# A 32-byte pool ahead of everything else on the right side of SBUF

## The chip, the core and the metric

The kernel runs on one core of a Trainium2 chip. The metric is device time in microseconds (us) of one execution. A core has five engines with queues of their own: TensorE (PE; its weight loads are shown apart as PEld), VectorE (DVE), ScalarE (ACT), GpSimd (POOL) and SyncE (SP, which issues nearly all DMAs here). On-chip memory, SBUF, is addressed by partition (128 of them) and by byte within the partition. A TensorE product has two operands in SBUF: the *stationary* one, which a LDWEIGHTS loads ahead of it (128 columns at most), and the *moving* one, which is streamed through (up to 512 columns here). In the profile's names `out<-a,b` of a MATMUL, a is the moving operand and b the stationary one.

## What is computed

One transformer block with adaptive layer norm over 2048 tokens of width 512: a sliding-window attention of 32 heads of 16 (window 256), then a gated feed-forward layer of inner width 1792.

```python
mod = (_silu(c) @ w_mod).reshape(c.shape[0], 6, 1, -1)
sa, ca, ga, sb, cb, gb = ...
h = _layernorm(x, axis=-1) * (1 + ca) + sa
x = x + ga * _A_ref(h, A_wqkv, A_wo)      # softmax(q k^T / 4, 0 <= i - j < 256) v, @ wo
h = _layernorm(x, axis=-1) * (1 + cb) + sb
x = x + gb * _B_ref(h, B_w1, B_w3, B_w2)  # (silu(h @ w1) * (h @ w3)) @ w2
```

## The kernel before

Everything is float32. To multiply at the fast rate, most operands are cut into a high and a low part of type float32r, and a product is three TensorE products: high by high, low by high, high by low. Nearly all products stream 512 columns past 128 stationary ones.

The work goes in four stages:

- Until about 95 us: layer norm, transposes, the value projection (line 703: stationary `hT`, the normed input; moving `wvh`/`wvl`, the weights) and the first query and key projections.
- Until about 467 us: attention, in 32 units (8 query-key blocks of a group of heads times 4 blocks of 512 tokens). Query and key projection is line 518 (stationary `wq`, moving `hT`), the scores for the running maximum line 574 and the scores proper line 931 (both operands in the tile `ring`), the product with the values line 892.
- Until about 539 us: the output projection (line 1315: stationary `o` or `x1b`, moving `wo`), the second layer norm and its transposes.
- The rest: the feed-forward layer. It is run in two halves of 1024 tokens and seven passes each, 14 passes in all. A pass makes two times seven products of the up and gate projection by a Strassen-like scheme (line 1579; six TensorE products of 512 columns each, so 84 in a pass: stationary the pass's weights, moving the tiles `b`) and eight products of the down projection (line 1673; six each, so 48 in a pass: stationary the gated activations, moving `w2`).

The order of each engine's instructions is fixed before the program runs: a planner in the kernel (class `Sched`, with tables of offsets) deals the operations out, and they are issued in that order on each engine. Places in SBUF don't enter into it.

SBUF is filled from two sides. Pools without `side` grow from the low addresses, pools with `side="right"` from the top down. Within a pool each tile begins on a multiple of 32 bytes. The right side holds the pool `a1` (opened first, at the top), and below it `hp` with `hT`, later replaced by `xp`. In the built program the large tiles then begin as follows, as bytes modulo 128 (and modulo 512) of their partition:

| tiles | side | used as | mod 128 | mod 512 |
|---|---|---|---|---|
| `ring`, `vS`, `b`, `w`, `w2`, `t`, `g`, `e` | left | scores, values, feed-forward | 64 | 448 |
| `wvh`, `wvl`, `pt`, `sm`, `jb`, `os` | left | value weights, probabilities | 64 | 64 or 448 |
| `hT`; later `x1a`, `x1b`, `wo`, `o` | right | normed input; residual, weights, attention output | 96 | 96 |
| `qk0`..`qk2`, `qkr`, `wq00`..`wq11`, `wqr` (pool `a1`) | right | queries, keys, their weights; later the gated activations | 96 | 96 |
| `junk` (pool `a1`) | right | unread output of line 581 | 32 | |

A column of a moving operand and a block of 128 stationary columns always begin a multiple of 512 bytes into these tiles, so the table's byte is that of both operands of every product of lines 518, 574, 703, 931, 1315, 1579 and 1673.

The weights of the feed-forward passes sit in two sets of two tiles, used in turn (`load_w`: `s = (half * NP + p) % 2`). Set 0 is `w` in the pool `fp`, on the left; set 1 takes over the places of `wo` and `o` in `xp`, on the right (`second_open`), and is shown by the profile under these names. So seven of the 14 passes have their up-projection weights on the left and seven on the right, while the moving tiles `b` are on the left. In the down projection the stationary activations lie in `a1` on the right under the names `wq`, `qk`, `qkr` (in the last pass half of them in `e` on the left), and the moving `w2`, or in the last pass `w`, is on the left.

The two lines around the change, 411 and 412, open the pool of PSUM and the first pool of the right side.

Of the kernel before, what the change touches and what calls it, by code (L numbers as in the profile page):

```python
# [8 lines left out]
F32 = mybir.dt.float32  # L9
# [9 lines left out]
P = 128  # L19
# [349 lines left out]
def block_kernel(ctx: ExitStack, tc: tile.TileContext, x, wqk, wv, wo, w13, w2, c, crow, wmod, wmodt, out):  # L369
# [39 lines left out]
        return hT[:, i, k, lo:lo + n]  # L409

    psA = ctx.enter_context(tc.tile_pool(name="psA", bufs=1, space=PSUM))
    a1 = ctx.enter_context(tc.tile_pool(name="a1", bufs=1, side="right", reuse_waits="tile"))

    def ps(b):
# [1395 lines left out]
```

## Time and profile before

| | before |
|---|---|
| three runs, us | 956.42, 956.73, 955.26 |
| median, us | 956.42 |
| the profiled execution: time, us | 956.27 |
| its span, first to last instruction, us | 954.6 |
| granted TensorE clock | 0.998 |
| busy, share of the span: DVE, ACT, POOL | 77%, 59%, 52% |
| mean DMA rate over the span | 148 GB/s |

The profile gives busy time by engine, a chain of work that ended last (followed back from the last instruction, each step to what released it), groups of instructions by line and tile, and busy time in chosen windows. The ends of matmuls are modelled, and a product's shown length overlaps the next one's (389 ns are shown where products follow each other every 226.7), so how fast products follow each other is read from the chain, whose pieces abut. A piece is shown as its start, its length and `engine tile line xN`, all in us.

### The profile page before, as it was taken

Reading aid. Unit: us, or ns where it says so; the run is one execution under the profiler, and the core shown is the slowest. Engines: PE = TensorE matmul, PEld = TensorE weight load, DVE = VectorE, ACT = ScalarE, POOL = GpSimd, SP = SyncE. Lnnn points to the kernel's source line nnn. Section 1 sums busy time; section 2 is a strip of 40 time slices with the busy share of each in tenths; the row PEclk is TensorE's granted clock in tenths of the full one; section 3 lists DMA queues with packets and bytes.
Section 4 is the critical chain, followed back from the end, with each engine's and each line's share of the span. In section 5 each row is a group of like instructions: output and inputs, shape, how many; then the busy total and the mean of one; then the engine's idle time right before and its main releaser. Section 6 shows DMA issues by size and latency. Waiting matters only on the chain.

```text
span 954.6 us, 17091 instructions
## 1 busy us (share of the span) xinstructions
PE 937.3 (98%) x5296; PEld 714.9 (75%) x5296; DVE 734.3 (77%) x2065; ACT 561.1 (59%) x1263; POOL 498.9 (52%) x721
## 2 busy tenths in 40 slices
PE   8999999999999999998999999999999999999998
PEld 4678777777777677775688788888888888888886
DVE  8884989898989898998468765666679766667555
ACT  6533878787878787876779833433456333433230
POOL 3230877787878686867544655444866222221320
PEclk9999999999999999999999999999999999999999
DMA  9521444444544444437893555466684421322002
GB/s 327 191 73 40 132 170 146 147 145 147 167 159 146 146 146 145 135 129 232 240 277 101 176 162 191 137 185 221 221 279 144 149 82 57 99 84 76 23 23 88
DMA packets 81561, 141.64 MB, mean 148 GB/s; under 512 B 10555, under 2 KB 23227, under 8 KB 81470
## 3 DMA queue, kind: packets, MB, share of 16 engines
q1 hardware_dynamic: 81180, 140.29, 45.4%
q8 instruction: 42, 0.69, 0.3%
q14 instruction: 49, 0.40, 0.1%
q10 hardware_dynamic: 290, 0.27, 0.1%
HBM read 85.73 MB, written 34.61 MB: 126 GB/s over the span
## 4 chain that ended last, share of the span: by engine, by line
PE 86%; POOL 4%; DVE 3%; DMA 3%; ACT 2%; issue 1%; SPq 1%; POOLq 0%; ACTq 0%; DVEq 0%
PE st L1579 12%; PE mx L1579 10%; PE pj L518 8%; PE mx L574 7%; PE st L931 7%; PE mx L1673 7%; PE po L892 7%; PE st L1673 5%; PE pj L1579 3%; PE po L1579 3%; PE mx L703 2%; PE po L1673 2%; PE st L1315 2%; PE pj L1673 2%; PE mx L1315 2%; PE st L703 2%
## 5 line engine op out<-in xcount | busy, mean ns | idle before, releaser
L581 DVE CUSTOM_DVE_ANT_0 junk<-mx,mskq 128x384 bf16<-128x384 f32 (+1 forms) x482 | 242.1, 528 | 23.8 <-PE mx L574 22.3
L931 PE MATMUL st<-ring 100*128 100x384 f32 (+2 forms) x484 | 146.2, 343 | 1.0 <-ACT pt L952 0.4
L574 PE MATMUL mx<-ring 96*128 96x384 f32 (+2 forms) x482 | 144.6, 340 | 1.7 <-ACT pt L943 0.6
L959 POOL TENSOR_SCALAR_AFFINE_SELECT pt<-pt 128x256 f32<-128x256 f32 x268 | 108.7, 408 | 51.7 <-ACT pt L952 38.3
L518 PE MATMUL pj<-hT,wq 128*128 128x512 f32 x384 | 132.1, 403 | 0.0
L952 ACT ACTIVATE pt<-st 128x256 f32<-128x256 f32 x255 | 91.4, 387 | 36.6 <-DVE st L949 28.5
L574 PEld LDWEIGHTS mx<-ring 96*128 96x128 f32 x482 | 88.0, 189 | 31.1 <-DVE mt L581 21.1
L931 PEld LDWEIGHTS st<-ring 100*128 100x128 f32 x484 | 90.2, 189 | 18.8 <-issue 6.7
L1623 POOL TENSOR_TENSOR t<-t,t 128x512 f32<-128x512 f32 x28 | 41.6, 1487 | 115.5 <-DVE t L1611 108.4
L892 PE MATMUL po<-pt,vS 128*17 128x256 f32 (+2 forms) x1408 | 97.4, 387 | 2.7 <-ACT os L999 1.1
L536 POOL TENSOR_TENSOR qk<-qkr,qk 128x512 fp32r<-128x512 f32 x64 | 82.9, 1295 | 10.4 <-ACT qkr L524 9.0
L1170 POOL TENSOR_TENSOR w<-w,w 128x512 fp32r<-128x512 f32 (+2 forms) x35 | 51.1, 1471 | 59.0 <-ACT w L1169 58.5
L1611 DVE TENSOR_TENSOR t<-st,t 128x512 f32<-128x512 f32 x55 | 37.9, 690 | 51.4 <-PE st L1579 38.5
L518 PEld LDWEIGHTS pj<-hT,wq 128*128 128x128 f32 x384 | 71.3, 189 | 7.7 <-issue 0.9
L949 DVE COPY_PREDICATED st<-later,st 128x128 f32<-128x128 uint8 x255 | 68.8, 292 | 7.9 <-PE st L931 4.7
L892 PEld LDWEIGHTS po<-pt,vS 128*17 128x17 f32 x1408 | 32.3, 96 | 48.5 <-issue 19.3
L1579 PE MATMUL st<-b,w 128*128 128x512 f32 x234 | 59.1, 391 | 0.0
L943 ACT ACTIVATE pt<-st 128x384 f32<-128x384 f32 (+2 forms) x113 | 47.1, 433 | 14.9 <-DVE st L939 13.7
L976 POOL TENSOR_SCALAR_AFFINE_SELECT sm<-sm 128x256 f32<-128x256 f32 x109 | 42.1, 409 | 24.1 <-ACT sm L966 20.0
L1579 PE MATMUL mx<-b,w 128*128 128x512 f32 x204 | 51.7, 391 | 0.0
L1579 PEld LDWEIGHTS st<-b,w 128*128 128x128 f32 x234 | 43.9, 188 | 9.5
L1651 ACT ACTIVATE qkr<-g 128x512 fp32r<-128x512 f32 x13 | 8.2, 633 | 66.5 <-DVE g L1607 66.5
(349 smaller groups left out, 2139.7 us busy)
## 6 DMA issues: line engine op xcount, KB each, us to landing
ring<-qk SPq DMA_DIRECT2D x192, 128.0 KB
o_dr<-os SPq DMA_DIRECT2D x32, 256.0 KB
w<-wsum SPq DMA_DIRECT2D x14, 512.0 KB
w<-w2g SPq DMA_DIRECT2D x14, 512.0 KB
jb<-in_w SPq DMA_DIRECT2D x24, 256.0 KB
vS<-in_wmodt SPq DMA_DIRECT2D x22, 256.0 KB
wraw<-in_w SPq DMA_DIRECT2D x7, 768.0 KB
w<-wraw SPq DMA_DIRECT2D x14, 384.0 KB
```

Source lines behind the costliest of these rows:

```text
L518: nc.tensor.matmul(v["ps"], WQ[g][w][:, n // 3], hTp(i, n // 3, b * BT, BT), start=(n == 0), stop=(n == 3 * KC - 1))
L536: nc.gpsimd.tensor_tensor(out=v[n], in0=v["raw"], in1=v[1].bitcast(F32), op=ALU.subtract)
L574: nc.tensor.matmul(v[i][:, :n], queries(NS, a, gq, 1), keys(NS, hh, a, k0, gq + 1 - k0), start=True, stop=True)
L581: nc.vector.tensor_tensor_reduce(out=junk[:, :n], in0=v[i][:, :n], in1=mskq[:, 3 * P - n:], scale=1.0, scalar=-3e38, op0=ALU.add, op1=ALU. ...
L892: nc.tensor.matmul(po[32 * i:32 * i + DH + 1, qb * P:(qb + nq) * P], vS[:, kb, 4 * g + i], pts[i // 2][:, i % 2, c0:c0 + nq], start=first, ...
L931: nc.tensor.matmul(ps[:, :nq], keys(NM, hh, a, kb, 1), queries(NM, a, kb, nq), start=True, stop=not plus)
L949: nc.vector.copy_predicated(ps[:, 0], later, ps[:, 2])
L952: nc.scalar.activation(pt_of(j, a)[:, hh, :2], v[j, a, hh][:, :2], AF.Exp, scale=SCALE)
L959: nc.gpsimd.affine_select(out=pt[:, :, 2 * m], in_=pt[:, :, 0], **w)
L1170: sch.op(eng, lambda: on_eng(eng).tensor_tensor(out=lo(), in0=src(), in1=hi().bitcast(F32), op=ALU.subtract), tt(eng, n), key, kl + kh, kl ...
L1579: nc.tensor.matmul(ps(bk), WT[s, n][w][:, col], BB[t, k][r], start=start and c == 0, stop=stop and c == 5, skip_group_check=True)
L1673: nc.tensor.matmul(ps(bk), tiles[hk + (h,)][:, i * P:(i + 1) * P], w2_of(last, y, f), start=(m == 0), stop=(m == 5))
```

## The change

Ahead of `a1` a pool named `edge` is opened on the right side, with one tile of 8 float32 numbers, 32 bytes in each partition. Nothing reads or writes it.

```diff
     psA = ctx.enter_context(tc.tile_pool(name="psA", bufs=1, space=PSUM))
+
+    ctx.enter_context(tc.tile_pool(name="edge", bufs=1, side="right")).tile([P, 8], F32, name="edge")
     a1 = ctx.enter_context(tc.tile_pool(name="a1", bufs=1, side="right", reuse_waits="tile"))
```

Every tile of the right side moves down by 32 bytes: from 96 to 64 modulo 128 for the large ones, and from 32 to 0 for `junk`. The left side stays where it is. No instruction, no order and no wait on a semaphore changes, only the addresses of right-side operands. The large tiles of both sides then begin at byte 64 modulo 128. Modulo 512, the right side goes from 96 to 64, so that a right-side tile stands 128 bytes from `b`, `w` and `ring`, where it stood 160 from them; `hT` stands 0 bytes from `wvh` and `wvl`, where it stood 32 from them. Line numbers of the changed kernel are larger by two behind line 411.

## The prediction

> **What bounds the kernel now.** First the page: how busy TensorE is, and how much of the chain of waits is its own.
>
> ```profile
> PE 937.3 (98%) x5296; PEld 714.9 (75%) x5296; DVE 734.3 (77%) x2065; ACT 561.1 (59%) x1263; POOL 498.9 (52%) x721
> PE 86%; POOL 4%; DVE 3%; DMA 3%; ACT 2%; issue 1%; SPq 1%; POOLq 0%; ACTq 0%; DVEq 0%
> ```
>
> TensorE leaves some 17 us of the span idle, so a change that moves no instruction can gain much only by making TensorE's products follow each other faster. Where it is fully busy is read from windows (length, busy us and count by engine, granted clock, DMA share, GB/s):
>
> ```profile
> 25.00:95.00 70.00, 69.08 (x316) 51.52 (x314) 51.11 (x143) 30.20 (x50) 13.09 (x11) 1.00 0.30 96
> 200.00:300.00 100.00, 99.33 (x773) 71.91 (x765) 91.23 (x390) 79.85 (x228) 75.97 (x140) 1.00 0.47 151
> 600.00:700.00 100.00, 100.00 (x440) 81.11 (x439) 67.27 (x87) 40.47 (x65) 52.71 (x53) 1.00 0.63 206
> 700.00:800.00 100.00, 100.00 (x433) 81.07 (x432) 75.03 (x95) 48.43 (x79) 41.95 (x26) 1.00 0.43 143
> 800.00:905.00 105.00, 105.00 (x455) 85.09 (x455) 69.24 (x93) 36.22 (x57) 24.73 (x18) 1.00 0.21 64
> ```
>
> In the feed-forward layer TensorE has no idle time, at full clock, and no other engine is above 75% (the third busy column is DVE's). In attention DVE is at 91% too. So the feed-forward layer ends when TensorE is through, and the pace of one product is what counts there. That pace stands in the chain of waits. Its pieces around 694 us, where a pass with weights on the right ends and one with weights on the left begins:
>
> ```profile
> 690.26 1.40 PE st L1579 x6
> 694.46 1.39 PE st L1579 x6
> 695.85 1.37 PE pj L1579 x6
> 697.22 1.36 PE mx L1579 x6
> 698.58 1.36 PE po L1579 x6
> 710.83 1.40 PE pj L1673 x6
> ```
>
> Six products of the same shape take 1.40 us on one side of 694 us and 1.36 after it: 233.3 and 226.7 ns each. The groups by tile say what differs (mean ns behind the busy time; 162 ns of it overlap the next product):
>
> ```profile
> L1579 PE MATMUL st<-b,w 128*128 128x512 f32 x234 | 59.1, 391 | 0.0
> L1579 PE MATMUL st<-b,o 128*128 128x512 f32 x132 | 34.2, 395 | 0.0
> L1673 PE MATMUL mx<-w,wq 128*128 128x512 f32 x144 | 37.0, 395 | 0.0
> L1673 PE MATMUL mx<-w,e 128*128 128x512 f32 x5 | 1.3, 392 | 0.0
> L1315 PE MATMUL st<-wo,x1b 128*128 128x512 f32 x12 | 3.0, 389 | 0.0
> L1579 PEld LDWEIGHTS st<-b,w 128*128 128x128 f32 x234 | 43.9, 188 | 9.5
> L1579 PEld LDWEIGHTS st<-b,o 128*128 128x128 f32 x132 | 24.8, 188 | 6.0
> ```
>
> It isn't the line: line 1579 has both paces, by its weights `w` (left) or `o` (right), and line 1673 too, by `wq` (right) or `e` (left). It isn't the right side as such: line 1315 has both operands on the right, and is the fastest. What goes with the slow pace is that the two operands lie on different sides, 64 and 96 modulo 128. The weight load itself takes 188 ns either way; it runs under the product ahead of it, so that product's stream is what is held up. Two more places of the chain agree: line 1315, both operands on the right, and the last down projection, where the first piece has right-side activations and the second has `e`.
>
> ```profile
> 475.62 2.72 PE mx L1315 x12
> 936.41 2.80 PE mx L1673 x12
> 940.60 1.38 PE mx L1673 x6
> ```
>
> 2.72 over 12 is 226.7 again, 2.80 over 12 is 233.3.
>
> **The change part by part.** It makes both sides equal modulo 128. The counts of products whose operands are now on two sides come from windows by tile or line: of line 1579 those that read `wo`, then `o`, then all of line 1673.
>
> ```profile
> 539.00:955.00 416.00, 69.97 (x294) 1.00 0.41 133
> 539.00:955.00 416.00, 73.92 (x294) 1.00 0.41 133
> 539.00:955.00 416.00, 167.22 (x672) 1.00 0.41 133
> ```
>
> Of the 672, 20 read `e` (four groups of five as in the row above), so 588 + 652 = 1240 products go from 233.3 to 226.7 ns: 1240 x 6.67 ns = **8.3 us**, all on the path.
>
> One thing must hold for that. The two operands will not be at equal bytes modulo 512 as in line 1315, but 128 apart. No row here has the weights of a 512-column stream 128 bytes off. The nearest is the value projection, 32 apart modulo 512 (`hT` against `wvh`), where the feed-forward layer is 160 apart:
>
> ```profile
> 86.11 4.20 PE st L703 x18
> by line: PE mx L703 33.3%; PE st L703 21.6%; PE pj L518 9.7%; PE st L730 5.4%; PE st L574 4.4%; PE st L683 4.4%; PE mx L730 3.8%; PE mx L683 3.8%; DVE hT L697 3.5%; PE mx L574 3.1%; ACT L943 1.8%; ACT vS L707 1.6%; ACT hT L692 1.1%; ACT h L
> ```
>
> 4.20 over 18 is 233.3. So 32 and 160 bytes apart cost the same, and adding 128 changed nothing; I take it that 0 and 128 are alike as well. The ends if not: no gain at all, or a loss as large as the gain.
>
> The same rows price the **value projection**: 54.9% of the 70 us from 25 to 95 us is line 703 on the chain, 38.4 us or 165 products, and 165 x 6.67 = 1.1 us. That stage also waits for DVE and ACT, so I take 0.7, between 0 and 1.1.
>
> **Run-ins** on the left: after each change of side the pace takes a few products to settle (1.39, 1.37, then 1.36 above), which is why `b,w` has a mean of 391 and not 389. 2 ns x 588 = 1.2 us at most; stalls will cause run-ins too, so I take 0.4, from 0.
>
> **Attention.** Here the order mixes lines 518, 574 and 931, and runs are too short for a settled pace.
>
> ```profile
> 135.69 0.69 PE pj L518 x3
> 139.78 0.24 PE pj L518
> L518 PE MATMUL pj<-hT,wq 128*128 128x512 f32 x384 | 132.1, 403 | 0.0
> L931 PE MATMUL st<-ring 100*128 100x384 f32 (+2 forms) x484 | 146.2, 343 | 1.0 <-ACT pt L952 0.4
> L574 PE MATMUL mx<-ring 96*128 96x384 f32 (+2 forms) x482 | 144.6, 340 | 1.7 <-ACT pt L943 0.6
> ```
>
> Line 518, both operands on the right, takes 230 to 240 ns here although its sides agree, so no clean gain can be read. If all 384 products settled at 226.7 ns, 384 x 6.7 = 2.6 us; if each of the 966 products of lines 574 and 931 were held up by 6.7, a loss of 6.4 us. I take a gain of 0.2: the products next to those of line 518 lose a difference of side, the others keep what they have.
>
> **Other engines and DMA.** The same shapes on the two sides:
>
> ```profile
> L1678 DVE TENSOR_TENSOR x1a<-mx,x1a 128x512 f32<-128x512 f32 x25 | 17.2, 688 | 6.7 <-PE mx L1673 6.5
> L1611 DVE TENSOR_TENSOR t<-mx,t 128x512 f32<-128x512 f32 x35 | 24.1, 689 | 23.8 <-PE mx L1579 22.8 <-ACT t L1618 0.4 <-ACT w L1169 0.3
> L1169 ACT ACTIVATE w<-w 128x1024 fp32r<-128x1024 f32 x14 | 14.7, 1051 | 1.5 <-DMA w<-wsum 1.5
> L1169 ACT ACTIVATE wo<-wo 128x1024 fp32r<-128x1024 f32 x7 | 7.4, 1055 | 4.0 <-DMA wo<-wsum 4.0
> L536 POOL TENSOR_TENSOR qk<-qkr,qk 128x512 fp32r<-128x512 f32 x64 | 82.9, 1295 | 10.4 <-ACT qkr L524 9.0
> L1060 POOL TENSOR_TENSOR jb<-jb,wqr 128x512 f32<-128x512 f32 x16 | 20.6, 1287 | 12.3 <-PE st L931 5.9 <-PE mx L574 3.0 <-PE pj L518 1.7
> ```
>
> 688 on the right and 689 on the left, 1051 and 1055, and 1287 for POOL with one operand on each side against 1295 on one: no place matters to them within 1%, and they hide under TensorE. DMAs have 3% of the chain, 28.6 us; if starting 32 bytes off cost 32 of each 2048-byte row, that is 0.45 us. Both at nothing, the bound kept.
>
> **New waits.** TensorE's waits in the feed-forward layer today are one row:
>
> ```profile
> PE po L1579 <- ACT t L1618: 0.4, 1, 0.4
> ```
>
> With TensorE 2% faster over 410 us, the others still have a quarter of their time, but the order is fixed and some results will now come late: the weight cuts (DMA, then ACT, then DVE or POOL) and the DVE additions of line 1611. I put 0.6 us to that, some two waits like this one, from 0 to 5.6 (one of 0.4 in each of the 14 passes).
>
> Sum: 8.3 + 0.7 + 0.4 + 0.2 - 0.6 = 9.0 us. The profiled execution took 956.27 us (span 954.6 and 1.7 around it); less 9.0 that is 947.3, and as it was 0.15 under the median of the runs, 947.4.
>
> The Trainium skill speaks against all this: the page "SBUF — State Buffer", section "Who interferes with whom", gives TensorE two independent read ports, one for the moving operand and one for LDWEIGHTS, and says that PE never waits on anyone. By that rule the change would be worth 0 and the time 956.4; the pace of 1.40 against 1.36 us for equal products disagrees.
>
> **The rivals.**
>
> *The period is longer than 128 bytes* (or place isn't the cause). Then the feed-forward products, 128 apart, stay at 233.3 ns, and only the value projection, exactly aligned, gains its 0.7: 955.7. For it: the only clean rows are at 0 modulo 512. Against it: 32 and 160 apart cost the same. 9%.
>
> *TensorE's lead is given back.* The products speed up, but the additions of line 1611 or the weight cuts come late once in every pass, and 5.6 of the 9.6 us before waits is lost: 956.4 - 4.0 = 952.4. For it: DVE at 75% from 700 to 800 us, DMA at 63% from 600 to 700. Against it: 0.4 us of waits today. 15%.
>
> *The new distance is worse than the old.* If the collision of the two read streams has a phase, 128 bytes may hit it twice as hard: another 6.67 ns for each of the 1240 products, 956.4 + 8.3 = 964.7. It decides as soon as six products with right-side weights take more than 1.40 us. For it: products on the same side in attention are not clean either (0.70 for three). Against it: the two unequal distances known cost the same, 233.3 ns. 5%.
>
> **How the numbers follow.** The forecast has 71%, with a range of its own from 945.6 to 949.5. Faster by over 0.2% (1.9 us, about what a measurement of this kernel can tell from no change) is the forecast and the second rival, 86%; within it the first rival, 9%; slower the third, 5%. The range for 8 in 10 goes from 945.0 (no new waits, value projection and run-ins in full, and a third of line 518's bound: 956.4 - 8.3 - 1.1 - 1.2 - 0.9 = 944.9) to 952.8, just over the second rival.
>
> **What would show it.** In the chain after, six products of lines 1581 and 1675 take 1.36 us whatever their tiles, and groups `b,o`, `b,wo`, `w,wq` have means near 389 to 391; a pass of the feed-forward layer with right-side weights is as short as one with left-side weights, but for the down projection. Eighteen products of the value projection take 4.08. DVE, ACT, POOL and LDWEIGHTS keep their means. The forecast is wrong if `b,o` stays at 395, or if it falls and TensorE's idle time in that stage grows by several us.

## The result, and the profile after

| | before | the change |
|---|---|---|
| median, us | 956.58 | 954.46 |
| lowest to highest of 20 runs each, us | 955.26 to 958.29 | 952.52 to 956.20 |
| the profiled execution: time (span), us | 956.27 (954.6) | 954.43 (952.7) |

The ratio is 0.9978, with a 95% interval from 0.9971 to 0.9984. So the change makes the kernel 2.1 us faster, 0.22%, where 9.0 were forecast; 954.46 lies above the range of 945.0 to 952.8.

The page first: busy time of the engines, and the chain by engine.

```profile
PE 936.7 (98%) x5296; PEld 715.5 (75%) x5296; DVE 734.2 (77%) x2065; ACT 560.8 (59%) x1263; POOL 497.6 (52%) x721
PE 86%; POOL 4%; DVE 4%; DMA 2%; ACT 2%; issue 2%; SPq 1%; POOLq 0%; DVEq 0%; ACTq 0%
```

TensorE's busy time fell by 0.6 us, and no other engine's by more than 1.3. Two windows in the feed-forward layer, where 440 and 433 products stood in 100 us before:

```profile
600.00:700.00 100.00, 100.00 (x443) 81.72 (x442) 67.66 (x88) 39.92 (x63) 52.92 (x53) 1.00 0.64 208
700.00:800.00 100.00, 100.00 (x435) 81.52 (x434) 76.00 (x96) 48.74 (x78) 42.31 (x26) 1.00 0.44 141
```

TensorE is still without a gap at full clock, and gets through two or three products more in 100 us. The chain of waits of the changed kernel, from the value projection to the last product:

```profile
86.87 4.12 PE st L705 x18
516.86 2.05 PE mx L1317 x9
662.86 2.79 PE mx L1581 x12
678.20 2.78 PE mx L1675 x12
690.74 1.40 PE mx L1675 x6
692.13 1.40 PE st L1675 x6
693.53 1.36 PE st L1581 x6
694.90 1.36 PE pj L1581 x6
945.67 2.81 PE mx L1675 x12
948.48 0.02 issue
```

Twelve products with operands on two sides took 2.80 us before and take 2.78 or 2.79 now: some 232 ns each, not 226.7. Only behind 693.5 us, with weights on the left, is the pace 1.36 for six, as before. The value projection, whose operands now begin at the same byte, did get the full pace but for its first few products: 4.12 us for 18, where it had 4.20. Two rows give the feed-forward layer its length: it begins where the last piece of the output projection ends (516.86 + 2.05 = 518.91) and ends with TensorE's last product at 948.48, which makes 429.57 us. The same rows of the chain before:

```profile
517.22 2.04 PE mx L1315 x9
947.53 2.82 PE mx L1673 x12
950.35 0.02 issue
```

There it is 950.35 - 519.26 = 431.09 us. The layer gained 1.52 us of the 8.1 forecast for it (8.3, and 0.4 of run-ins, less 0.6 of waits), the time ahead of it 0.35.

The groups by tile, of the changed kernel:

```profile
L1581 PE MATMUL st<-b,w 128*128 128x512 f32 x234 | 58.9, 390 | 0.0
L1581 PE MATMUL st<-b,o 128*128 128x512 f32 x132 | 34.1, 395 | 0.0
L1675 PE MATMUL mx<-w,wq 128*128 128x512 f32 x144 | 36.9, 395 | 0.0
L1581 PEld LDWEIGHTS st<-b,o 128*128 128x128 f32 x132 | 24.9, 188 | 5.8
L1680 DVE TENSOR_TENSOR x1a<-mx,x1a 128x512 f32<-128x512 f32 x25 | 17.2, 688 | 6.6 <-PE mx L1675 6.5
L1062 POOL TENSOR_TENSOR jb<-jb,wqr 128x512 f32<-128x512 f32 x16 | 20.5, 1284 | 13.0 <-PE mx L576 4.7 <-PE pj L520 2.3 <-DMA wsum<-jb 2.3
```

The groups `b,o` and `w,wq` stayed at 395 ns. This is what the prediction named as the sign that it is wrong. Weight loads, VectorE and GpSimd kept their means, as it said.

### The profile page after: what moved, and what is told of

Its sections match the earlier page's. It is cut to its first block, busy times and chain, and to the rows that moved or that the text cites. A ratio compares the mean times of both kernels' runs of the same rounds, so it can differ in the third digit from the quotient of the medians.

```text
span 952.7 us, 17091 instructions
## 1 busy us (share of the span) xinstructions
PE 936.7 (98%) x5296; PEld 715.5 (75%) x5296; DVE 734.2 (77%) x2065; ACT 560.8 (59%) x1263; POOL 497.6 (52%) x721
## 4 chain that ended last, share of the span: by engine, by line
PE 86%; POOL 4%; DVE 4%; DMA 2%; ACT 2%; issue 2%; SPq 1%; POOLq 0%; DVEq 0%; ACTq 0%
PE st L1581 12%; PE mx L1581 10%; PE pj L520 8%; PE mx L576 7%; PE st L933 7%; PE mx L1675 7%; PE po L894 7%; PE st L1675 5%; PE pj L1581 3%; PE po L1581 3%; PE mx L705 2%; PE po L1675 2%; PE st L1317 2%; PE pj L1675 2%; PE mx L1317 2%; PE st L705 2%
## 5 line engine op out<-in xcount | busy, mean ns | idle before, releaser
L954 ACT ACTIVATE pt<-st 128x256 f32<-128x256 f32 x255 | 91.3, 386 | 36.1 <-DVE st L951 28.2
```

The source lines that it names most:

```text
L954: nc.scalar.activation(pt_of(j, a)[:, hh, :2], v[j, a, hh][:, :2], AF.Exp, scale=SCALE)
```

## The experiments

Five theories stood at the beginning. A: the full pace comes when the moving and the stationary operand begin at the same byte modulo 256 or 512, not 128. B: it hangs on where the right-side tile lies, not on its distance from the other. C: the pace could be had, but another engine would then be late. D: an odd multiple of 32 bytes is what hurts, so that 64 apart would be quick. E: the cost is graded by distance. In what follows the distance is the stationary operand's first byte minus the moving one's, and the length of the feed-forward layer is worked out from the chain as above.

**The right side at the left's byte modulo 512.** The tile of the change with 160 bytes in place of 32:

```diff
-    ctx.enter_context(tc.tile_pool(name="edge", bufs=1, side="right")).tile([P, 8], F32, name="edge")
+    ctx.enter_context(tc.tile_pool(name="edge", bufs=1, side="right")).tile([P, 40], F32, name="edge")
```

> A pad of 160 bytes instead of 32: right-side tiles at 448 modulo 512, as ring, b, w and w2. Theory A (a product runs at full pace when its moving and its stationary operand begin at the same byte modulo 256 or 512, and 128 is not enough): six products of line 1581 or 1675 take 1.36 us with right-side weights too, where the 32-byte pad left 1.39 to 1.40; 1240 products x 5.7 ns = 7.1 us and some 0.4 of run-ins come off 954.5, and the value projection, now 128 bytes apart, goes back to about 232 ns and gives 0.7 back: 947 to 948.5. Rival B (the pace depends on the absolute place of the right-side tile, or on its side): 1.39 to 1.40 stays, 954 to 956. Rival C (pace comes, but other engines become late): 1.36 where TensorE runs, several us of new idle time of TensorE behind 539 us, 950 to 952.

Measured: 946.62 us (five runs, 944.84 to 947.0) against 956.98 of before on the same chip, ratio 0.9885 (0.9868 to 0.9901). Its chain of waits:

```profile
86.90 4.17 PE st L705 x18
516.73 2.04 PE mx L1317 x9
663.22 2.72 PE st L1581 x12
675.46 2.72 PE mx L1675 x12
690.42 1.36 PE st L1581 x6
940.68 0.02 issue
```

and its groups by tile:

```profile
L1581 PE MATMUL st<-b,w 128*128 128x512 f32 x234 | 58.7, 389 | 0.0
L1581 PE MATMUL st<-b,o 128*128 128x512 f32 x132 | 33.3, 389 | 0.0
L1675 PE MATMUL mx<-w,wq 128*128 128x512 f32 x144 | 36.1, 389 | 0.0
```

All three groups, those with operands on two sides too, are at 389 ns, and every piece of twelve takes 2.72 us. The layer is 940.68 - 518.77 = 421.91 us long, 9.18 less than before. Theory C falls: with TensorE 2.1% faster there, nothing came late enough to take any of it back. The value projection, now 384 bytes apart, is at 4.17 for 18.

**The left side moved in its place.** No tile on the right, and 160 bytes on the left:

```diff
+    cst.tile([P, 40], F32, name="edge")
     ident = cst.tile([P, P], F32, name="ident")
```

> No pad on the right; 160 bytes ahead of all tiles on the left instead, so that ring, b, w, w2 go from 448 to 96 modulo 512, where the right side is. Theory A (only the distance of the two operands counts): the same as the 160-byte pad on the right, 1.36 us per six and 947 to 949. Rival B (the absolute place of the right-side tile): right-side tiles stand where they stood before, so 1.40 and about 956.

Measured: 946.12 us (one run). Chain of waits:

```profile
516.25 2.04 PE mx L1316 x9
662.75 2.72 PE st L1580 x12
940.20 0.02 issue
```

The large tiles of both sides are now at byte 96 modulo 512, where the right side stood before the change, and the layer is again 940.20 - 518.29 = 421.91 us. So it is the distance that counts, and not the place: B falls.

**Other distances.** The tile of 160 bytes on the right with 96, 64 and 128 bytes instead (`[P, 24]`, `[P, 16]`, `[P, 32]`).

> Pad of 96 bytes: the feed-forward operands are 64 bytes apart modulo 512, those of the value projection 64 the other way (448). Theory A: both slow, 231 to 235 ns per product, 955 to 957. Rival D (what hurts is an odd multiple of 32 bytes, and 128 is a bad case of its own): 64 apart is fast, 1.36 us per six in the feed-forward layer, 947 to 949.

> Pad of 64 bytes: the feed-forward operands are 96 bytes apart modulo 512, those of the value projection 32 the other way (480). Theory A: both slow, 231 to 235 ns per product, 955 to 957. Rival E (the cost is graded by the distance, least near 0): the value projection, 32 from equal, is between 227 and 233 ns, and the feed-forward layer is worse than with 32 bytes of pad.

> The tile is 128 bytes: right-side tiles at 480 modulo 512, 32 from the feed-forward layer's moving tiles, and hT 416 (that is, -96) from wvh. Theory A (full pace only where moving and stationary operand begin at the same byte modulo 256 or 512): feed-forward products with operands on two sides stay at 232 to 234 ns, value projection too, time 955 to 958. Rival F (only multiples of 128 hurt less, every other distance costs the same): the same time, so this run only adds a distance to the table; 232 or less at 32 bytes apart, with time under 953, would say that nearness counts after all.

Measured: 956.24, 957.16 and 957.49 us (one run each), all like before. These tiles put the operands of the feed-forward layer 64, 96 and 32 bytes apart. Of the chain of waits, a piece of the value projection and one of the feed-forward layer; with 96 bytes:

```profile
86.87 4.13 PE st L705 x18
666.49 2.80 PE st L1581 x12
```

with 64 bytes:

```profile
86.58 4.19 PE st L705 x18
667.02 2.81 PE st L1581 x12
```

with 128 bytes:

```profile
87.41 4.20 PE st L705 x18
668.15 2.80 PE st L1581 x12
```

A feed-forward layer 64 bytes apart is as slow as before: D falls. The layer's length, read from these chains as above, is 431.09 us at 64 bytes, 431.50 at 96 and 430.40 at 32, the smallest step that these pools can make. At 160 it was 431.09, and equal bytes give 421.91: the first 32 bytes bring nearly the whole cost, and so E falls. The rival F named there, that multiples of 128 alone cost less, is right by a little: the change, 128 bytes apart, has 429.57, the shortest of the unequal ones, by 0.8 us.

**256 bytes apart.** This tells a period of 256 bytes from one of 512. No room is left for 256 bytes more on the right, so the tile of 160 bytes was kept and the second buffer of `junk` taken away, which raises all large right-side tiles by 768 bytes, to 192 modulo 512:

```diff
-            junk = a1.tile([P, 3 * P], BF16, name="junk", bufs=2)
+            junk = a1.tile([P, 3 * P], BF16, name="junk", bufs=1)
```

> The 160-byte tile, and junk with one buffer in place of two, which raises the other right-side tiles by 768 bytes: they then begin at 192 modulo 512, 256 from the feed-forward layer's moving tiles, and hT 128 from wvh. Theory A256 (period of 256 bytes): feed-forward products at 226.7 ns, 946 to 948 us. Theory A512 (period of 512 bytes): they stay at 229 to 234 ns, 952 to 958 us. The single buffer of junk is written by one engine in order and should cost under 0.3 us.

Measured: 970.40 us (four runs), ratio 1.0151 (1.0134 to 1.0168): slower than before by 13.8 us, which neither theory expected. The chain of waits tells two things apart:

```profile
87.93 4.17 PE st L705 x18
538.76 2.04 PE mx L1317 x9
685.30 2.72 PE st L1581 x12
962.76 0.02 issue
```

The feed-forward layer has the full pace, 962.76 - 540.80 = 421.96 us. So equal bytes modulo 256 are enough. A shorter period of 128, 64 or 32 bytes is excluded, since the layer is slow at each of these distances. The loss lies ahead of it: the output projection ends 22 us later than with the tile of 160 bytes alone.

**The control for it.** `junk` with one buffer again, but a tile of 928 bytes (`[P, 232]`) ahead of it, so that all large right-side tiles stand where the tile of 160 bytes had put them.

> A control for the kernel with 256 bytes between the operands, whose total rose although its feed-forward products ran at 226.7 ns: junk with one buffer as there, but a tile of 928 bytes ahead of it, so that all other right-side tiles stand where they stood with the 160-byte tile (448 modulo 512, equal to the left). If the rise comes from the single buffer of junk (each of the 482 operations that write it waits for the one before it): 968 to 972 us again, and attention as long as there. If it comes from the place (the operands 256 apart, or hT at 192): 946 to 948 us.

Measured: 969.26 us (four runs), ratio 1.0123 (1.0107 to 1.0140). The chain of waits, and then the group that writes `junk`:

```profile
540.10 2.04 PE mx L1317 x9
686.57 2.72 PE st L1581 x12
964.02 0.02 issue
```

```profile
L583 DVE CUSTOM_DVE_ANT_0 junk<-mx,mskq 128x384 bf16<-128x384 f32 (+1 forms) x482 | 255.4, 530 | 38.2 <-PE mx L576 8.7 <-PE st L933 0.3
```

The same group with two buffers, in the kernel with the tile of 160 bytes:

```profile
L583 DVE CUSTOM_DVE_ANT_0 junk<-mx,mskq 128x384 bf16<-128x384 f32 (+1 forms) x482 | 242.0, 528 | 24.1 <-PE mx L576 22.6
```

The layer is 421.88 us long, and the loss ahead of it is there again: the output projection ends 23.4 us later than with the tile of 160 bytes, where it was 22.0. So the loss is the price of the single buffer, and not of 256 bytes between the operands. VectorE's idle time ahead of this group grew from 24.1 to 38.2 us, and of that only 9.0 is put down to TensorE where 22.6 was. What the rest is shows where two of these operations follow each other. With two buffers, in the kernel with 160 bytes as it was run again further below (start and length in us):

```profile
300.69 0.55 DVE L583 CUSTOM_DVE_ANT_0 junk<-mx,mskq 128x384 bf16<-128x384 f32 x1
301.17 0.55 DVE L583 CUSTOM_DVE_ANT_0 junk<-mx,mskq 128x384 bf16<-128x384 f32 x1
```

and with one, in the control:

```profile
301.45 0.56 DVE L583 CUSTOM_DVE_ANT_0 junk<-mx,mskq 128x384 bf16<-128x384 f32 x1
302.16 0.56 DVE L583 CUSTOM_DVE_ANT_0 junk<-mx,mskq 128x384 bf16<-128x384 f32 x1
```

With two buffers the second begins 0.48 us behind the first and before the first has ended; with one it begins 0.71 us behind it, 0.15 after the first has ended. Over the 236 such pairs of each trace whose first is 384 wide, the median step is 477 and 709 ns. The built program has the reason: with one buffer 476 of the 512 operations that write `junk` wait on VectorE's own semaphore for the one just before, with two buffers 383 wait for the one before that. This falls into the stage in which VectorE was 91% busy before, where there is little room to make it good. How the 22 us add up from these steps was not worked out.

**Everything at the same byte.** The tile of 160 bytes, and on the left the value weights moved behind the small tiles of their pool and 32 bytes, so that they begin at 448 modulo 512 too:

```diff
-    wvh = p0.tile([P, KC, D], F32R, name="wvh")
-    wvl = p0.tile([P, KC, D], F32R, name="wvl")
...
+    p0.tile([P, 8], F32, name="gap")
+    wvh = p0.tile([P, KC, D], F32R, name="wvh")
+    wvl = p0.tile([P, KC, D], F32R, name="wvl")
```

> The 160-byte tile, and on the left side wvh and wvl placed behind the small tiles of their pool and a gap of 32 bytes, so that they too begin at 448 modulo 512 and the value projection has its operands at equal bytes as well. Theory A: feed-forward as with the 160-byte tile alone, and 165 products of the value projection at 226.7 in place of 232.4 ns, 0.9 us less at most; since that stage also waits for other engines and the start for DMA, 0.3 to 0.9 us below the 160-byte tile alone, 945.5 to 946.5 us. Rival G (value projection is bound by the additions and copies around it): its products at 226.7, but the same total as with the 160-byte tile alone, within 0.2 us.

Beside it the tile of 160 bytes alone ran again:

> The 160-byte tile alone again, for comparison with the run before on the same chip: 946 to 947.5 us, feed-forward products all at 226.7 ns, value projection at 232.4.

Measured: 946.50 us (four runs), ratio 0.9894 (0.9879 to 0.9908), and for the tile alone 947.34 (four runs), 0.9903 (0.9888 to 0.9918). The chain of waits of the first:

```profile
86.46 4.12 PE st L706 x18
515.97 2.04 PE mx L1318 x9
662.48 2.72 PE st L1582 x12
939.93 0.02 issue
```

The value projection has its pace, 4.12 in place of 4.17 for 18, which over 165 products is 0.5 us; the feed-forward layer is 421.92 us. Between the two kernels 0.8 us lie on the same chip, and only 0.1 between this one and the first five runs of the tile alone. That they differ in total is not settled, so the rival G named there, that the value projection's pace is no gain in total, stays open. Both beat the kernel before and the change.

## Why the prediction went wrong

**The distances together.** One row for each distance modulo 256, from the pieces of 12 or 18 products quoted here and in the prediction, with the length of the feed-forward layer. A piece is shown to 0.01 us, which is 0.8 ns a product of twelve; the layer's length is the finer measure.

| distance modulo 256 | feed-forward layer, us | feed-forward, ns a product | value projection, ns a product |
|---|---|---|---|
| 0 | 421.88 to 421.96 | 226.7 (2.72 of 12), at 0 and at 256 | 228.9 (4.12 of 18, first products included) |
| 32 | 430.40 | 233.3 (2.80) | 233.3 (4.20), before |
| 64 | 431.09 | 233.3 (2.80) | |
| 96 | 431.50 | 234.2 (2.81) | |
| 128 | 429.57 | 232.5 (2.79), the change | 231.7 (4.17), at 128 and at 384 |
| 160 | 431.09 | 233.3 (2.80), before | 233.3 (4.20), at 416 |
| 192 | | | 229.4 (4.13), at 448 |
| 224 | | | 232.8 (4.19), at 480 |

Where two stages or two distances fall into one row, they agree within 1 ns, apart from the run-in at distance 0. One distance in eight has the full pace. 192, which was read in the value projection alone, comes within 0.5 ns of what equal bytes give in that stage. The other six lie within 2.5 ns of each other.

**The step that failed** is this one: "So 32 and 160 bytes apart cost the same, and adding 128 changed nothing; I take it that 0 and 128 are alike as well." Both rows it used were slow ones. Two slow rows 128 bytes apart show only that both are slow; a period is shown by a quick row that comes back. At 128 a product takes 232.5 ns, so the term of 8.3 us came to (233.3 - 232.5) x 1240, some 1.0 us; by the rounding of the pieces this is anything up to 2, and the whole layer gained 1.52. The change moves the right side to a place that is equal modulo 128 and not modulo 256.

**What held.** That the pace of one product bounds the layer, and that unequal first bytes of the two operands are what slows it: with the distance at 0 the layer is 9.18 us shorter, where 8.3 for the products and 0.4 for the run-ins were worked out. The total of 946.62 to 947.34 there is close to the forecast of 947.4, reached with 160 bytes and not with 32. That it comes so close is in part luck: the layer gave 1.1 us more than the 8.1 forecast for it, and the 0.7 for a value projection with equal bytes isn't in it.

**Run-ins** were taken as 0.4. In the changed kernel the group `b,w` went from 391 to 390 ns; how the layer's 1.52 us divide between run-ins and two-sided products can't be told from pieces of this rounding. With all operands at distance 0 it is at 389 and the layer's gain exceeds the 8.3 by 0.9: the term was small by half.

**The value projection** gained what was forecast: 0.08 us of 18 products, which over 165 is 0.7. Yet only 0.35 us was left of it where the feed-forward layer begins. In the eleven profiles the last piece of the value projection ends anywhere from 91.3 to 95.1 us, in the two of the kernel with 160 bytes at 93.2 and 94.1, which is more than any such gain. The granted clock of the first 25 us differs too, 1.00 in the profile before and 0.93 in the one after. One profile of each can't tell where the other part went.

**New waits** were taken as -0.6, between 0 and -5.6. None came: the layer's one wait of TensorE that the prediction shows, 0.4 us ahead of 539 us, is 0.5 in the changed kernel, and behind 539 us neither kernel has one in the list. With the full pace the layer's five lengths lie between 421.88 and 421.96 us. The second rival, a lead that is given back, is refuted by these kernels, in which there was a lead to give.

**Attention** was taken as 0.2 with wide bounds. Its groups did not move: line 518, now 520, has 403 ns before and after.

**The rivals.** The first, a period longer than 128 bytes, is what happened; it gave 955.7 because it left the feed-forward products at exactly 233.3, and with the 1.5 us that the layer gained it would have been 954.2. It was given 9%, though its only counter-argument was the step above. The third, a worse distance, did not come: no distance tried costs over 234.2 ns. The rule of the Trainium skill, page "SBUF — State Buffer", section "Who interferes with whom", by which TensorE waits for no one at its two read ports, gives 956.4 at every distance. Here the kernels with distance 0 are 9.2 us shorter in one stage with the same instructions, and for that the rule leaves no room: as far as these runs go, it doesn't hold between the two operands of a product stream. What in the chip has a period of 256 bytes isn't shown by any of these runs.

## What to carry to other kernels

Where TensorE is without a gap and each of its products loads its own weights, as here with 128 by 128 of them and 512 columns of float32r, look at the pace of equal products by tile, and let the moving and the stationary operand begin at the same byte modulo 256 of their partition. Here a pad of 160 bytes ahead of either side did it. Before forecasting from a period, find a quick row on either side of it: two slow rows at its distance say only that both are slow.

## What was not expected of the hardware

Of the eight distances in steps of 32 bytes the seven unequal ones are not quite alike: in the value projection 192 has 229.4 ns where equal bytes have 228.9, and the other six have 231.7 to 234.2. Whether 192 is as good in the feed-forward layer wasn't tried.

A buffer that nothing reads can carry a price: with one in place of two for the output of 482 VectorE operations the kernel takes 22 us more (969.26 against 947.34), 46 ns for each on average, although they run on one engine in order. Two such operations with no wait between them overlap a little, 0.07 us in the rows above; the wait on the one before takes that away and leaves VectorE idle for some 0.15 us. The wait is the program's: the kernels with one buffer have 89 instructions more (17180 against 17091 in the trace), in the built program all of them waits of VectorE on a semaphore.
